# Query–key products in quarter tiles of the PE array, two steps per visit

## The chip, the cores and the metric

The kernel runs on one core of a Trainium2 chip. The metric is the device time of one launch in microseconds, as the median of three runs. Five engines work side by side, each through its own queue in order: PE (TensorE) multiplies matrices, with its weight loads shown apart as PEld; DVE (VectorE), ACT (ScalarE) and POOL (GpSimd) work on rows of numbers; SP (SyncE) issues the transfers. Matrix products land in PSUM, which has eight banks; everything else stands in SBUF.

## The reference

Four sequences of 576 positions go through windowed attention with eight heads of width 64 (a query sees the 128 latest keys, with a bias that falls with distance), then through a soft mixture of eight experts with four slots each, then through a dense layer with a squared ReLU. The change touches the attention alone.

```python
scores = scale * np.matmul(q, k.transpose(0, 1, 3, 2))
mask = (rel >= 0) & (rel < window)                  # rel = query position - key position
scores = np.where(mask, scores + bias[None], -1000000000.0)
scores = scores - np.max(scores, axis=-1, keepdims=True)
attn = np.exp(scores)
attn = attn / (np.sum(attn, axis=-1, keepdims=True) + 1e-09)
x = np.matmul(attn, v)
...
d = softmax of x @ phi over all 2304 tokens (per slot)
slot_out[e] = relu((d.T @ x)[e] @ w1[e]) @ w2[e]
x = softmax of x @ phi over the 32 slots (per token) @ slot_out
h = relu(x @ w_in); out = h * h @ w_out
```

## The kernel before

**Units, chunks, steps.** A unit `u` is one sequence and one pair of heads; there are 16. Its 576 queries are cut into nine chunks `c` of 64. The two heads of a pair lie on partitions 0 to 63 and 64 to 127. One chunk sees at most 192 keys (64 in the first chunk, 128 in the second). A step `t` handles two chunks, so there are 72 steps, 4.5 for each unit; `info[2 * t + i]` names the chunk `i` of step `t`.

**The stages of a step**, each in a function of its name:

- `emit_S(t)`, L157 to L163: one product for each chunk. The stationary operand is `zq`, 128 by 128: the queries of head 0 in the upper left quarter, those of head 1 in the lower right one, and zeros in the other two, so that one product gives both heads. The result stands in one PSUM bank for the step, chunk 0 in columns 0 to 191, chunk 1 from column 256 on. There are three such banks (tag `S`). Every fp32 product is shown as two PE instructions.
- `emit_max(t)`, L165: on DVE, one custom instruction for each chunk adds the bias table `tbl`, writes the scores into one of five buffers `pbuf[t % 5]` and takes the row minimum of the negated scores.
- `emit_exp(t)`, L176: on ACT, the exponential with its row sum.
- `emit_add(t)` and `emit_norm(t)`, L183 to L194: DVE adds 1e-9 to the two sums and takes their reciprocals; POOL multiplies the two chunks by them.
- `emit_T(t)`, L198: PE turns the step's probabilities, up to two 128 by 128 transposes into a bank `tp` and one or two into a bank `tq`. Both come from the tag `T`, which has three banks and also holds `xb`, `X`, `Y` and `R`.
- `emit_evac(t, 0)` copies `tp` into `ptb` on ACT, `emit_evac(t, 1)` copies `tq` on DVE, mostly in two pieces (L235, L237).
- `emit_PV(u)`, L239: when a unit's blocks are there, PE multiplies them with the values, in two halves of 64 array columns (`xa`, `xb`). `emit_xT` copies the result on ACT; `emit_xn` turns it again (five transposes into `X` and `Y`, L279 and L281), copied by DVE (L283) and ACT. After each fourth unit come the router's products `L` (32-column tiles, L267 and L272, a bank of their own with the tag `B`) and the sums of its softmax (`emit_d0` to `emit_d4`).

**The order** is written out by hand in the loop over `t` (L394 to L426): in step `t` PE does `emit_S(t + 1)`, then `emit_T(t - LT)` with `LT = 3`, then a due `emit_PV`. DVE does `emit_max(t)`, `emit_add(t - 1)` with the reciprocal, then `emit_evac(t - 3, 1)`; ACT does `emit_evac(t - 3, 0)` and then `emit_exp(t)`. A tile is reused only when all its readers are through, so an engine that runs ahead waits there.

**Transfers.** All loads are issued on SP. When `emit_S` has passed a unit's last chunk, the queries and keys of unit `u + 2` are loaded into the buffers of unit `u` (two loads for the queries, one for each half, in pieces of 64 numbers, since `zq` has zeros in between; one for the keys), and then one expert weight of 1 MB into a ring of 19 (two weights at `u` 2 and 6). For unit 0 the host has laid out the zeros itself (`z0`).

After the attention come the expert products (L567, L659), which run on weights from that ring, and the dense layer (L692, L735).

## Time and profile before

| what | value |
|---|---|
| median of three runs | 422.15 us (421.33 to 423.01) |
| the profiled execution, own time | 423.25 us |
| its span in the trace | 421.5 us |
| attention loop, first `emit_PV` to last | 16.28 us to 137.74 us |
| expert products | 148.2 us to 178.7 us |
| granted TensorE clock over the span | 0.994 |

The page shows, for each engine, how long it was busy; a busy PE includes the pipeline's overlap, so how densely it works is read from the distance between the starts of its rows. The profiled execution took 1.1 us more than the median, so what is said of the span's parts holds for the median within that.

### The profile page before, as it was taken

To read this page: it belongs to the slowest core of one execution; us is meant where nothing else is said; L and a number is where in the kernel's file an instruction comes from. 1 tells how busy PE (TensorE), PEld (TensorE's weight loads), DVE (VectorE), ACT (ScalarE), POOL (GpSimd) and SP (SyncE) were. 2 spreads that over 40 slices of the span, in tenths; PEclk is the share of its full clock that TensorE was granted. 3 is DMA by queue.
4 is the path that set the end of the run, shared out by engine and by line. 5 is a ranking of instruction groups with operands and counts; after the bars stand their busy time and mean duration, and the time that the engine had idled before them with its cause. 6 is when DMAs were issued, how large, how long until landed. Compare 5 with 4: busy or idle time off the path is not lost.

```text
span 421.5 us, 7942 instructions
## 1 busy us (share of the span) xinstructions
PE 400.4 (95%) x2623; PEld 306.7 (73%) x2623; DVE 293.4 (70%) x966; ACT 249.7 (59%) x761; POOL 94.6 (22%) x193
## 2 busy tenths in 40 slices
PE   5999997999999999978999999999999999999996
PEld 4878866878867633356778788787878888888885
DVE  6887777778788426587868768677676676548445
ACT  3888876778777402057766766666666645435341
POOL 4445334244334010146112210111100000000000
PEclk9999999999999999999999999999999999999999
DMA  7979769869686799999602202000000012004004
GB/s 215 307 276 305 261 218 323 218 194 313 223 287 233 264 425 423 412 409 408 255 0 101 100 2 100 2 0 0 2 1 2 1 64 87 0 2 150 0 2 150
DMA packets 35514, 70.95 MB, mean 168 GB/s; under 512 B 19856, under 2 KB 21008, under 8 KB 31376
## 3 DMA queue, kind: packets, MB, share of 16 engines
q1 hardware_dynamic: 35328, 70.30, 47.7%
q8 instruction: 21, 0.34, 0.4%
q14 instruction: 21, 0.17, 0.1%
q10 hardware_dynamic: 144, 0.13, 0.1%
HBM read 65.70 MB, written 4.72 MB: 167 GB/s over the span
## 4 chain that ended last, share of the span: by engine, by line
PE 51%; DVE 2%; issue 1%; POOL 1%; ACT 1%; DVEq 0%; POOLq 0%
PE acc L735 45%; PE h L692 4%; PE MX L644 1%; DVE psum L753 1%; PE MY L650 1%; POOL arena_y L605 1%; DVE arena_y L621 1%; DVE arena_y L619 0%; ACT whl L637 0%; DVE Mst L653 0%; DVE arena_co L623 0%; ACT psum L745 0%; ACT siT L745 0%; DVE arena_gh L721 0%; DVEq L896 0%
## 5 line engine op out<-in xcount | busy, mean ns | idle before, releaser
L735 PE MATMUL acc<-whl,arena_gh 128*128 128x512 f32 x864 | 214.4, 396 | 2.3 <-DVE arena_gh L721 1.8
L735 PEld LDWEIGHTS acc<-whl,arena_gh 128*128 128x128 f32 x864 | 159.9, 189 | 34.8 <-issue 2.8
L721 DVE TENSOR_TENSOR arena_gh<-hT,arena_gh 128x384 fp32r<-128x384 f32 (+1 forms) x95 | 52.7, 555 | 38.5 <-ACT arena_gh L717 34.1
L194 POOL TENSOR_SCALAR p<-p,st 128x192 f32<-128x192 f32 (+1 forms) x142 | 56.1, 408 | 77.0 <-PE s L162 20.2
L704 ACT ACTIVATE acc<-h 128x384 f32<-128x384 f32 (+2 forms) x49 | 23.8, 485 | 75.0 <-PE h L692 75.0
L181 ACT ACTIVATE p<-p,st 128x192 f32<-128x192 f32 (+1 forms) x144 | 61.3, 428 | 8.0 <-DVE st L170 7.3
L162 PE MATMUL s<-kt,zq 128*128 128x192 f32 (+2 forms) x288 | 58.8, 328 | 7.4 <-DMA kt<-in_k_dram 7.0
L605 POOL TENSOR_SCALAR arena_y<-f 128x512 f32<-128x512 f32 x32 | 27.9, 875 | 120.7 <-DVE arena_cin L623 59.0
L162 PEld LDWEIGHTS s<-kt,zq 128*128 128x128 f32 x288 | 44.8, 195 | 10.1 <-DMA zq<-in_z_dram 4.6
L237 DVE COPY ptb<-tq 64x128 f32<-64x128 f32 x128 | 35.4, 281 | 22.1 <-PE tq L215 18.9
L170 DVE CUSTOM_DVE_ANT_0 p<-s,tbl 128x192 f32<-128x192 f32 (+1 forms) x144 | 41.6, 324 | 2.3 <-PE s L162 1.8
L235 ACT ACTIVATE ptb<-tp 128x256 f32<-128x256 f32 (+1 forms) x72 | 25.3, 351 | 19.4 <-PE tp L213 18.1
L247 PE MATMUL xa<-ptb,vt 128*64 128x256 f32 (+1 forms) x256 | 27.8, 359 | 0.0
L213 PE MATMUL tp<-cs,p 128*128 128x128 f32 x128 | 26.4, 277 | 1.3 <-DVE ptb L237 0.7
L181 ACT ACTIVATION_READ_ACCUMULATOR p<-p,st 128x1 f32 x144 | 27.2, 189 | 0.0
L692 PE MATMUL h<-cst_sb,Mst 128*128 128x384 f32 x96 | 25.2, 341 | 1.9 <-DVE Mst L653 1.8
L713 DVE TENSOR_TENSOR hT<-acc 128x384 f32<-128x384 f32 (+1 forms) x18 | 10.2, 566 | 23.4 <-ACT acc L704 23.4
L717 ACT ACTIVATE arena_gh<-acc 128x384 fp32r<-128x384 f32 (+2 forms) x49 | 24.9, 508 | 0.6
L717 ACT ACTIVATE arena_gh<-hT 128x384 fp32r<-128x384 f32 x48 | 24.9, 518 | 0.6
L621 DVE SCALAR_TENSOR_TENSOR arena_y<-f,arena_y 128x512 int32<-128x512 int32 x32 | 24.1, 753 | 1.1
L247 PEld LDWEIGHTS xa<-ptb,vt 128*64 128x64 f32 x256 | 17.0, 136 | 9.6 <-issue 2.4
L692 PEld LDWEIGHTS h<-cst_sb,Mst 128*128 128x128 f32 x96 | 18.1, 190 | 7.1 <-DVE Mst L653 3.3
(171 smaller groups left out, 475.3 us busy)
## 6 DMA issues: line engine op xcount, KB each, us to landing
w_w<-in_w_dram SPq DMA_DIRECT2D x32, 1024.0 KB, 8.1
f<-in_w_in_dram SPq DMA_DIRECT2D x16, 512.0 KB, 10.2
f<-in_w_out_dram SPq DMA_DIRECT2D x16, 512.0 KB, 10.2
vt<-in_v_dram SPq DMA_DIRECT2D x16, 320.0 KB, 6.2
zq<-in_q_dram SPq DMA_DIRECT2D x30, 144.0 KB, 4.3
kt<-in_k_dram SPq DMA_DIRECT2D x15, 288.0 KB, 4.4
out_dram<-psum SPq DMA_DIRECT2D x11, 256.0 KB, 2.1
out_dram<-xn_all SPq DMA_DIRECT2D x4, 256.0 KB, 2.1
```

The costliest lines, as they stand in the source:

```text
L162: pe.matmul(out=sb_t[t][:, 256 * i:256 * i + n], lhsT=zq[u % NQ][:, c].rearrange("p a b -> p (a b)"), rhs=kt_t[u][:, 64 * c + 64 - n:64 * ...
L170: dve.tensor_tensor_reduce(out=p, in0=sb_t[t][:, 256 * i:256 * i + n], in1=tbl[:, 192 * pr + 192 - n:192 * pr + 192], scale=-0.125, scalar ...
L181: act.activation(out=p, in_=p, func=AF.Exp, bias=st[:, i:i + 1], scale=-1.0, accum_out=st[:, 2 + i:3 + i])
L194: eng.tensor_scalar(out=p, in0=p, scalar1=st[:, 4 + i:5 + i], scalar2=0.0, op0=ALU.mult, op1=ALU.add)
L237: dve.tensor_copy(out=dst, in_=src)
L247: pe.matmul(out=out, lhsT=v_t[u][:, j, po:po + 64], rhs=pt[:, a:b, po:po + 64], start=(j == 0 or (j == 3 and a == 2)), stop=(j == 4 or (j ...
L605: pool.tensor_scalar(out=y[:, a].bitcast(F32), in0=t[:, a, :, 1].bitcast(F32), scalar1=2.0 ** -112, scalar2=0.0, op0=ALU.mult, op1=ALU.add)
L621: dve.scalar_tensor_tensor(out=y[:, h], in0=t[:, h, :, 1], scalar=-0x80000000, in1=y[:, h], op0=ALU.bitwise_and, op1=ALU.bitwise_or)
L692: pe.matmul(out=hb[hf][:, 0:HB], lhsT=Mst[:, 128 * f:128 * f + 128], rhs=cst_sb[:, c0:c0 + HB], start=True, stop=True)
L717: act.activation(out=lo_t[i][1][hf][:, 0, cl], in_=rbuf[hf][:, cl], func=AF.Square)
L721: eng.tensor_tensor(out=gh[hf][:, 1, cl], in0=g[hf][:, cl], in1=gh[hf][:, 0, cl].bitcast(F32), op=ALU.subtract)
L735: pe.matmul(out=acc_t[s], lhsT=gh[:, x, c0:c0 + 128], rhs=w[:, f % 2, y, :], start=(f in firsts and a == 0), stop=(f in lasts and a == 2))
```

## The change

`emit_S` is called in even steps alone, for two steps at once (four chunks), two steps ahead. The queries are loaded as they are (`qt`, 128 by 576), without zeros. Each chunk takes two products, one for each head, with a stationary operand of 64 by 64 in one quarter of the array: the rows of head `h`, and the columns `64 * (h ^ w)`. `w` is 0 or 1 by the chunk's place in `pbuf`; with `w = 1` the two heads come out swapped, and the result stands in the second bank of a pair. There are two pairs of banks instead of three single banks. The bias table gets a second, swapped copy, and `emit_PV` finds its columns through a new function `cols`.

The sums of two steps are added to and inverted in one DVE instruction each, over four columns, in even steps; POOL normalizes four chunks after that. `LT` becomes 4. The router's `L` takes its bank from the tag `T`, whose number stays three. The double weight loads move from `u` 2 and 6 to 7, 11 and 13, and one of the extra loads at the end of the attention comes two steps sooner.

```diff
-LT = 3
+LT = 4
...
-    NBUF = {"S": 3, "T": 3, "xa": 1, "B": 1}
+    NBUF = {"S": 1, "T": 3, "xa": 1}
...
+    def pair(name):
+        return psum[0].tile([128, 2, 512], F32, tag="S", name=name, bufs=2)
...
     def emit_S(t):
-        sb_t[t] = bank("S", "s")
-        st_t[t] = apool.tile([128, 6], F32, tag="st", name="st", bufs=4)
-        for i in range(2):
-            u, c, n, e = info[2 * t + i]
-            pe.matmul(out=sb_t[t][:, 256 * i:256 * i + n], lhsT=zq[u % NQ][:, c].rearrange("p a b -> p (a b)"),
-                      rhs=kt_t[u][:, 64 * c + 64 - n:64 * c + 64], start=True, stop=True)
+        sb_t[t] = sb_t[t + 1] = pair("s")
+        st_t[t] = st_t[t + 1] = apool.tile([128, 12], F32, tag="st", name="st", bufs=3)
+        for x in range(2):
+            for i in range(2):
+                u, c, n, e = info[2 * t + 2 * x + i]
+                w = e // 192
+                for h in range(2):
+                    r, o = 64 * h, 64 * (h ^ w)
+                    pe.matmul(out=sb_t[t][o:o + 64, w, 256 * x:256 * x + n], lhsT=qt_t[u][r:r + 64, 64 * c:64 * c + 64],
+                              rhs=kt_t[u][r:r + 64, 64 * c + 64 - n:64 * c + 64], start=True, stop=True,
+                              tile_position=(r, o), skip_group_check=True)
...
     def emit_add(t):
         st = st_t[t]
-        dve.tensor_scalar(out=st[:, 2:4], in0=st[:, 2:4], scalar1=1e-9, scalar2=None, op0=ALU.add)
+        dve.tensor_scalar(out=st[:, 4:8], in0=st[:, 4:8], scalar1=1e-9, scalar2=None, op0=ALU.add)
+        dve.reciprocal(out=st[:, 8:12], in_=st[:, 4:8])
...
+    def cols(u, j, h, a, b):
+        ap = ptb[:, jblk(u, j) + a:jblk(u, j) + b, 0:64]
+        same = u % 2 == 1 and j == 0 and a == 0
+        first = 64 * (1 - h) if same else 64 * h
+        step = 128 if same else 128 + 64 * (1 - 2 * h)
...
-            for a, b in ((0, 4),) if j < 3 else ((0, 2), (2, 3)) if j == 3 else ((0, 1),):
+            for a, b in ((0, 2), (2, 4)) if u % 2 and j == 0 else ((0, 4),) if j < 3 else ((0, 2), (2, 3)) if j == 3 else ((0, 1),):
...
-            L_t[b] = bank("B", "L")
+            L_t[b] = bank("T", "L")
...
-        if t + 1 < NS:
-            emit_S(t + 1)
-            for u, c, n, e in info[2 * t + 2:2 * t + 4]:
+        if t % 2 == 0 and t + 2 < NS:
+            emit_S(t + 2)
+            for u, c, n, e in info[2 * t + 4:2 * t + 8]:
                 if c == NCH - 1:
                     if u + NQ < NU:
                         load_q(u + NQ)
-                    for _ in range(2 if u in (2, 6) else 1):
+                        load_k(u + NQ)
+                    for _ in range(2 if u in (7, 11, 13) else 1):
                         load_next_w()
...
-        if 0 <= t - 1 < NS:
-            emit_add(t - 1)
+        if t % 2 == 0 and 0 < t <= NS:
+            emit_add(t - 2)
         if t < NS:
             emit_exp(t)
-        if 0 <= t - 1 < NS:
+        if t % 2 == 0 and 0 < t <= NS:
+            emit_norm(t - 2)
             emit_norm(t - 1)
...
-        if t == NS - 2:
+        if t == NS - 4:
             zt.close()
             load_extra(1)
```

How the order of PE changes is seen at the same place in the program, the second unit: first the kernel before. `s` is the product of queries and keys, `tp` and `tq` are the two banks of a step's transposes.

```order
L162 MATMUL s_564<-kt_394,zq0_90 128x192 x2
L213 MATMUL tp_568<-cs_66,p0_93 128x128 x2
L215 MATMUL tq_569<-cs_66,p0_93 128x128
L162 MATMUL s_584<-kt_394,zq0_90 128x192 x2
L213 MATMUL tp_588<-cs_66,p1_94 128x128 x2
L215 MATMUL tq_589<-cs_66,p1_94 128x128
L162 MATMUL s_604<-kt_394,zq0_90 128x192 x2
L213 MATMUL tp_608<-cs_66,p2_95 128x128 x2
L215 MATMUL tq_609<-cs_66,p2_95 128x128
```

And the changed kernel on PE, two steps with their visit and the next visit (`X` and `Y` are the transposes of a finished unit):

```order
L167 MATMUL s_596<-kt_456,qt_454 64x192 x2
L221 MATMUL tp_612<-cs_66,p1_92 128x128 x2
L223 MATMUL tq_613<-cs_66,p1_92 128x128
L221 MATMUL tp_630<-cs_66,p2_93 128x128 x2
L223 MATMUL tq_631<-cs_66,p2_93 128x128
L297 MATMUL X_642<-cs_66,xT2_99 128x128 x4
L299 MATMUL Y_647<-cs_66,xT2_99 128x128
L167 MATMUL s_651<-kt_456,qt_454 64x192 x8
```

Products and transposes alternated step by step; now eight products stand together, and the transposes of two steps follow one another with no product between them.

On DVE, before, the last chunk of the second unit and the first chunk of the third: one step (the ISA rows of 64 to 192 columns are the row minima, the narrow ones read their result out):

```order
L170 ISA p3_96,st_389<-s_388,tbl_92 128x192
L170 ISA st_389 128x1
L170 ISA p3_96,st_389<-s_388,tbl_92 128x64
L170 ISA st_389 128x1
L185 TENSOR_SCALAR st_360<-st_360 128x2
L189 RECIPROCAL st_360<-st_360 128x2
L237 COPY ptb_98<-tq_437 64x128 x2
```

And on DVE after the change, two steps, the same chunks and the two that follow:

```order
L176 ISA p3_94,st_332<-s_331,tbl_90 128x192
L176 ISA st_332 128x1
L176 ISA p3_94,st_332<-s_331,tbl_90 128x64
L176 ISA st_332 128x1
L245 COPY ptb_96<-tq_415 64x128
L176 ISA p4_95,st_378<-s_377,tbl_90 128x128
L176 ISA st_378 128x1
L176 ISA p4_95,st_378<-s_377,tbl_90 128x192
L176 ISA st_378 128x1
L192 TENSOR_SCALAR st_332<-st_332 128x4
L193 RECIPROCAL st_332<-st_332 128x4
L245 COPY ptb_96<-tq_461 64x128 x2
```

The pair of small instructions on the sums stands in every second step, and works on four columns; the copies of `tq` keep their place behind each step's minima.

## Rows read from the trace of the kernel before

**Rows 1.** The page, part 1: engine, busy us, share of the span, instructions.

```profile
PE 400.4 (95%) x2623; PEld 306.7 (73%) x2623; DVE 293.4 (70%) x966; ACT 249.7 (59%) x761; POOL 94.6 (22%) x193
```

**Rows 2.** Stretches: length, then each engine's busy us, clock, DMA share, GB/s.

```profile
16.28:31.35 15.07, 14.33 (x121) 12.09 (x121) 12.23 (x73) 12.33 (x52) 7.12 (x18) 1.00 0.88 283
64.53:73.61 9.08, 6.71 (x57) 5.51 (x56) 6.90 (x41) 6.10 (x27) 4.77 (x12) 1.00 1.07 322
16.28:137.74 121.46, 115.71 (x1055) 93.08 (x1054) 95.14 (x541) 92.64 (x386) 51.50 (x130) 1.00 0.81 259
148.20:180.00 31.80, 31.77 (x283) 11.03 (x283) 14.58 (x46) 4.81 (x12) 4.58 (x5) 1.00 1.01 419
200.00:422.00 222.00, 216.41 (x1052) 175.31 (x1050) 150.87 (x274) 126.45 (x285) 19.77 (x22) 1.00 0.13 49
```

**Rows 3.** Timeline of PE: start us, us until the last end, line, tiles, count.

```profile
102.46 0.38 PE L213 MATMUL tp<-cs,p 128*128 128x128 f32 x2
102.68 0.27 PE L215 MATMUL tq<-cs,p 128*128 128x128 f32 x1
102.79 0.82 PE L162 MATMUL s<-kt,zq 128*128 128x192 f32 x4
103.44 0.38 PE L213 MATMUL tp<-cs,p 128*128 128x128 f32 x2
103.66 0.27 PE L215 MATMUL tq<-cs,p 128*128 128x128 f32 x1
```

**Rows 4.** Timeline of DVE over the same steps (brackets: idle before, releaser).

```profile
102.99 0.59 DVE L237 COPY ptb<-tq 64x128 f32<-64x128 f32 x2 [0.94 <-PE tq L215]
103.50 0.34 DVE L170 CUSTOM_DVE_ANT_0 p<-s,tbl 128x192 f32<-128x192 f32 x1
...
103.78 0.34 DVE L170 CUSTOM_DVE_ANT_0 p<-s,tbl 128x192 f32<-128x192 f32 x1
...
104.06 0.16 DVE L185 TENSOR_SCALAR st<-st 128x2 f32<-128x2 f32 x1
...
104.44 0.59 DVE L237 COPY ptb<-tq 64x128 f32<-64x128 f32 x2
104.96 0.34 DVE L170 CUSTOM_DVE_ANT_0 p<-s,tbl 128x192 f32<-128x192 f32 x1
```

**Rows 5.** Timeline of ACT over the same steps: copy, then the second exponential.

```profile
102.88 0.38 ACT L235 ACTIVATE ptb<-tp 128x256 f32<-128x256 f32 x1 [0.58 <-PE tp L213]
...
103.88 0.37 ACT L235 ACTIVATE ptb<-tp 128x256 f32<-128x256 f32 x1
```

**Rows 6.** Timeline of PE around one product with the values.

```profile
64.32 0.27 PE L221 MATMUL tq<-cs,p 128*128 128x128 f32 x1
64.53 1.73 PE L247 MATMUL xa<-ptb,vt 128*64 128x256 f32 x16
66.09 0.40 PE L247 MATMUL xb<-ptb,vt 128*64 128x64 f32 x8
66.42 0.92 PE L162 MATMUL s<-kt,zq 128*128 128x192 f32 x4
67.17 0.38 PE L213 MATMUL tp<-cs,p 128*128 128x128 f32 x2
```

**Rows 7.** Timeline of PE around the router's products, four tiles of 32 columns.

```profile
42.46 1.08 PE L267 MATMUL L<-xT,phi_sb 128*32 128x128 f32 x32
43.36 0.61 PE L272 MATMUL L<-xT,phi_sb 128*32 128x64 f32 x8
```

**Rows 8.** Timeline of DVE: copy of a unit's transposes, and the next step.

```profile
98.45 0.69 DVE L283 COPY xn_all<-X 128x512 f32<-128x512 f32 x1
99.06 0.35 DVE L170 CUSTOM_DVE_ANT_0 p<-s,tbl 128x192 f32<-128x192 f32 x1
```

**Rows 9.** Timeline of PE: the long wait in the stretch 64.53 to 73.61.

```profile
73.05 0.41 PE L162 MATMUL s<-kt,zq 128*128 128x64 f32 x2 [2.10 <-DMA kt<-in_k_dram]
```

**Rows 10.** The page, part 3: packets of the whole span.

```profile
DMA packets 35514, 70.95 MB, mean 168 GB/s; under 512 B 19856, under 2 KB 21008, under 8 KB 31376
```

More of the change, by code (lines that the diff above doesn't have):

```diff
@@ L24, with attn_moe_relu2_kernel @@
 RING = 19
[L25 removed]
+LT = 4
 @with_exitstack
[L29 removed]
+def attn_moe_relu2_kernel(ctx: ExitStack, tc: tile.TileContext, q, k, v, phi, w1, w2, w_in, w_out, bias, cst, out):
     nc = tc.nc
@@ L94, in keep_warm @@
     def keep_warm(tag, n):
-        b = bank(tag, "warm")
+        b = bank(tag, "warm") if tag in NBUF else Sbank[1]
         for _ in range(n):
@@ L114, in attn_moe_relu2_kernel @@
     NQ = 2
-    zq = [zpool.tile([128, NCH, 2, 64], F32, name=f"zq{i}") for i in range(NQ)]
-    tbl = ppool.tile([128, 768], BF16, name="tbl")
+    tbl = ppool.tile([128, NPAIR, 2, 192], BF16, name="tbl")
     NP = 5
@@ L237, in emit_evac @@
                 dve.tensor_copy(out=dst, in_=src)
+    def cols(u, j, h, a, b):
[3 more added lines that the diff above has]
+        step = 128 if same else 128 + 64 * (1 - 2 * h)
+        dims = [[256, (b - a) // 2], [step, 2], [1, 64]] if b - a > 1 else [[1, 64]]
+        assert not same or b - a == 2
+        return bass.AP(tensor=ap.tensor, offset=ap.offset + first, ap=[list(ap.ap[0])] + dims)
     def emit_PV(u):
@@ L461, in attn_moe_relu2_kernel @@
     pool.memset(siT, 0.0)
-    W = bank("B", "W")
+    Sp = pair("sp")
+    Sbank = [Sp[:, 0], Sp[:, 1]]
+    W = pair("W")[:, 0]
     for bb in range(4):
         pe.transpose(W[:, 128 * bb:128 * bb + 128], lgT[:, bb, 0:128], ident)
-    G = bank("S", "G")
+    G = Sbank[0]
     pe.matmul(out=G[:, 0:4], lhsT=rep, rhs=bm, start=True, stop=True)
@@ L877, in _layout @@
     for pr in range(NPAIR):
-        slope = 2.0 ** -(2.0 * pr + p // 64 + 1.0)
-        bias[:, 192 * pr:192 * pr + 192] = np.where(ok, -8.0 * slope[:, None] * rel, -8.0e9)
+        for w in range(2):
+            slope = 2.0 ** -(2.0 * pr + (p // 64 ^ w) + 1.0)
+            bias[:, pr, w] = np.where(ok, -8.0 * slope[:, None] * rel, -8.0e9)
     cst[:, 0:128] = np.eye(128, dtype=np.float32)
```

67 lines of the change are left out of this document (28 added, 39 removed).

## The prediction

> **What bounds the kernel now.** I read the page's busy shares first, then the stretches, then the timeline of each engine inside the stretch that the change touches. PE is busy for 95% of the span [rows 1], but the span has three parts with different limits. In the expert products PE is full (31.77 of 31.80 us) while the transfers run at a share of 1.01, and in the dense part PE has 216.41 of 222 us [rows 2]; both begin when the attention ends, and no instruction of theirs changes. So the change is decided in the attention loop, 121.46 us from the first product with the values to the last, which is 67 steps [rows 2].
>
> There the row to look at is the stretch 16.28 to 31.35: nine steps, two units, without the router's work, in 15.07 us, or 1.67 us a step [rows 2]. What does an engine need for nine steps? On PE, from start to start, a step's products take 0.65 us (102.79 to 103.44), its two tp transposes 0.22 and tq 0.11 [rows 3]: 0.98 us. A unit's product with the values takes 1.89 us (64.53 to 66.42) and 0.10 us more before it, since 0.21 lies between tq and xa where 0.11 lies between tq and s [rows 3, 6]. Its five transposes X and Y take 5 x 0.11 = 0.55. Nine steps hold two of each: 9 x 0.98 + 2 x 1.99 + 2 x 0.55 = 13.9 us. On DVE a step is 1.46 us (103.50 to 104.96) [rows 4], and a unit's copy of X 0.61 (98.45 to 99.06) [rows 8]: 9 x 1.46 + 2 x 0.61 = 14.4 us, some 0.4 less for the short first chunks. So **two engines are nearly full at once**, PE with 13.9 and DVE with 14.0 of 15.07 us. ACT is busy for 12.33 us, POOL for 7.12 [rows 2]. A cut on PE alone would change little; this change cuts both.
>
> **Products in quarters.** Two steps' products cost 2 x 0.65 = 1.30 us of PE. Four products of 64 by 64 at a time would need four passes of a quarter of that 0.65, 0.65 us a visit. That tiles work at the same time is seen for columns: 32 instructions of the router, four tiles of 32 columns, start within 0.90 us (42.46 to 43.36), four of them per 0.11 us, the time of one transpose of the same width [rows 3, 7]; and the two halves of xa run as pairs [rows 6]. No row of before shows tiles that split the array's rows. I take full overlap, 0.65, with 1.30 as the other end. What is new is two changes of tile shape for each visit: the 0.10 us before xa, and 0.10 more on the first group of s after xb (0.75 us from 66.42 to 67.17, against 0.65) [rows 3, 6]. That makes 0.20 to 0.40 us a visit; I take 0.30. A visit then costs 0.95 us, 0.35 less, and nine steps (4.5 visits) 1.6 us less of PE. Where a product with the values stands next to a visit, one change of shape was there already; the odd units' extra pair of short products leaves the columns as they are.
>
> **Sums of two steps.** One TENSOR_SCALAR and RECIPROCAL in two steps fall away, 0.38 us (104.06 to 104.44) [rows 4]: 1.7 us of DVE in nine steps. Wider by two columns costs nothing that a row shows. POOL gets its four multiplications in one go; it has half its time free, and the lag of four steps leaves two steps between the sums and the transposes, as before.
>
> If all else flowed as before, both full engines would lose 1.6 to 1.7 of 15.07 us: 67 / 9 x 1.65 = **12 us** at most.
>
> **The new closed loop.** The visit of step t needs a free pair of banks, so the minima of step t - 1 must be through. On DVE these stand behind the copies of the tq that PE made right after the visit before. PE waits at the visit, with the transposes of two steps and a due product with the values queued behind it; ACT waits for their tp, DVE for their tq. The loop, from the first product of a visit: transposes at 0.65 + 0.20 = 0.85; tq 0.22 later, 1.07; its copy begins 0.31 after tq (102.68 to 102.99), 1.38; the two copies take 0.51, 1.89; the two minima end 0.62 after the first starts (103.50 to 103.78 + 0.34), 2.51 [rows 3, 4]; about 0.1 to wake PE: 2.6 us. Against 2 x 1.46 on DVE that is a gain, but the rest adds to it. With a product with the values in the two steps PE needs 0.85 + 0.33 + 1.99 + 0.33 + 0.10 = 3.6 us, and 3.8 when it comes after the second step: there the transposes of two steps stand together, and the second tq takes the bank of the first tp, which ACT gives back 0.31 + 0.38 us after that [rows 5], some 0.3 late. With X and Y the copy of X (0.61) comes into the loop, or Y waits for a bank that ACT copies behind its exponentials (a copy and two short exponentials take 1.00 us, 102.88 to 103.88) [rows 5, 8]: 3.2 to 3.4. Nine steps are two of the first kind, two of the second and half a plain one: 2 x 3.7 + 2 x 3.3 + 0.5 x 2.6 = 15.3, less 0.3 for the short chunks: 15.0 us. **By this sum nothing is gained.**
>
> How far may such a sum be trusted? Made the same way for before (two steps with the values 2.97, two with X 2.07, five plain ones 1.46, less 0.3) it gives 17.1, and 15.07 were measured: engines work ahead into each other's steps and take back 12%. After the change less of that is possible, since the loop closes every two steps. I take a third of it, 4%, off: 14.35 us, 0.7 less than before, times 67 / 9: **-5.3 us**. The ends are -12 (above) and -0.5 (nothing taken back).
>
> **The rest.** The router's L now holds one of the three T banks, so X and Y of that step wait; on the other side L lies in the loop's shadow. A batch's softmax puts DVE work as long as X's copy (0.69) into the loop. Three batches, taken together **+0.8 us**, from -2 to +3. In the stretch 64.53 to 73.61 PE waited 2.10 us for keys while the transfers had a share of 1.07 [rows 2, 9], behind two weights that SP had issued one after the other. The double loads move, and the queries, until now in 256-byte pieces (19856 of 35514 packets are under 512 bytes [rows 10]), come in whole rows. I take **-1.9 us**, from 0 to -2.1; at u 7 the keys of unit 10 are still queued behind two weights. One step more of lag at the start against fewer bytes before the second visit, and a bank less at the end: **+0.7 us**, from -1 to +2. A nineteenth weight in the ring hides behind a full PE. PE's longer waits should not cost clock: it stayed at 1.00 in the stretch with the 2.10 us [rows 2].
>
> The sum: -5.3 + 0.8 - 1.9 + 0.7 = -5.7 us. The profiled execution would go from 423.25 to 417.6, the median from 422.15 to **416.4 us**.
>
> **The rivals.** *Quarters take turns* (the change does not do what it says). A visit would take 1.30 + 0.30, 0.65 more, straight into the loop: 36 x 0.65 = 23 us, some 435 to 440 us. For it: no row shows row tiles, and the quarters of one chunk write the same bank. The Trainium skill, "TensorEngine Tiling (Array Packing)", section "Restrictions and Gotchas", says that different row tiles cannot access the same PSUM bank simultaneously; by that rule the time is the one just given. No run here shows it; the skill's page "TensorE: Matmul & The Clock Gate", Part 3, on the other hand reports 10.6 times the speed for 16 tiles in rows and columns. Against it: column tiles that share a bank overlap fully [rows 7].
>
> *The loop is longer than its rows* (slower). Place: PE at the visit, waiting for DVE's minima, and at the second tq, waiting for ACT. If nothing is taken back, the changes of shape cost their dear 0.40 (0.45 in nine steps) and the bank's 0.3 us is lost in each plain or X pair too, nine steps take 15.9, and the end is 422.15 + 6.2 - 0.4 = 428 us. It decides from 15.13 us for nine steps on (with 0.4 gained elsewhere). *Nothing is taken back, but nothing more is lost:* 15.0 us, 421 us. *The engines' sums hold:* -12 - 0.4, 410 us.
>
> **How the numbers follow.** The forecast, 412 to 420 us: 0.48. Engines' sums, under 412: 0.12. About no change, 420 to 424: 0.18. Loop longer, 424 to 430: 0.14. Quarters in turn: 0.08. A measurement of this kernel can tell about 0.5%, 2.1 us, from no change: faster 0.60, same 0.18, slower 0.22. The range, 408 to 429, leaves out the quarters in turn and the outer ends of the two cases beside it.
>
> **What would show it.** Right: sixteen instructions of s within about 0.75 us on PE, waits of PE on DVE's minima that did not exist before, nine steps near 14.4 us, the stretch from the first to the last product with the values near 116 us, no wait of 2 us for keys, and expert and dense parts as long as before. Wrong: s spread over 1.3 us a visit; PE as full as before, which would mean that the loop has slack; or PE idle for over 1 us in plain pairs, which would mean that ACT's banks and not DVE set the loop.

## The result and the profile after

| | median, us | runs, us |
|---|---|---|
| the kernel before, same chip | 422.31 | 421.04 to 424.96 |
| the changed kernel | 426.09 | 423.52 to 430.48 |
| ratio | 1.0097 | 95% interval 1.007 to 1.0123 |

The change makes the kernel 0.97% slower. The forecast was 416.4 us, faster by 1.4%: the sign was wrong, though the time lies within the range 408 to 429. The profiled execution of the changed kernel took 425.98 us with a span of 424.2; that of the kernel before had 423.25 and 421.5. So the two traces differ by 2.7 us, and the medians by 3.8.

The page of the changed kernel, parts 1 and 2, answers to [rows 1, 10]:

```profile
PE 395.6 (93%) x2943; PEld 285.5 (67%) x2943; DVE 286.9 (68%) x894; ACT 249.2 (59%) x761; POOL 93.5 (22%) x191
...
DMA packets 19771, 70.87 MB, mean 167 GB/s; under 512 B 2192, under 2 KB 3344, under 8 KB 15632
```

PE has 4.8 us less to do, DVE 6.5 us less, and of 19856 packets under 512 bytes 2192 are left. The work became less, as forecast; the time did not. **Where it went** is read from one event that both kernels have, the first instruction of each product with the values (`xa`), and from the stages behind:

| event | before | after | later by |
|---|---|---|---|
| first `xa` | 16.28 | 19.29 | 3.01 |
| third | 31.35 | 36.34 | 4.99 |
| seventh | 64.53 | 69.54 | 5.01 |
| eleventh | 99.81 | 102.75 | 2.94 |
| fifteenth | 133.16 | 134.72 | 1.56 |
| sixteenth | 137.74 | 139.43 | 1.69 |
| first expert product | 148.22 | 150.45 | 2.23 |
| first product of the dense layer | 183.37 | 185.59 | 2.22 |
| end of the span | 421.5 | 424.2 | 2.7 |

The table says three things. All of the loss is there by the third unit, 5 us. From the third to the seventh, four units or 18 steps in the steady state, the two kernels take the same time. Later 2.1 us come back between the seventh and the eleventh, where the kernel before waits for keys [rows 9], and 1.4 us in the last units: the way from the fourteenth to the fifteenth takes 7.87 us, where the same place four units before takes 9.12. There the last visit, at 128.75, is already behind, and PE has only transposes and values left. The way from the last `xa` to the first expert product is 0.5 us longer, the dense layer 0.5.

**The steady state.** Stretches from the third to the seventh `xa`: first the kernel before, then the changed one (columns as in [rows 2]).

```profile
31.35:64.53 33.18, 32.24 (x294) 26.06 (x293) 26.07 (x150) 25.48 (x109) 14.21 (x36) 1.00 0.83 265
```

```profile
36.34:69.54 33.20, 30.50 (x373) 20.17 (x372) 24.31 (x131) 25.42 (x107) 14.08 (x36) 1.00 0.72 237
```

PE and DVE each lost 1.7 us of work in 33, and the stretch is as long as before. Idle time took the place of work. The changed kernel's PE behind a product with the values shows both what was gained and what it cost:

```profile
62.31 0.88 PE L167 MATMUL s<-kt,qt 64*64 64x192 f32 x16
63.12 0.44 PE L221 MATMUL tp<-cs,p 128*128 128x128 f32 x2
63.40 0.27 PE L223 MATMUL tq<-cs,p 128*128 128x128 f32 x1
63.51 0.38 PE L221 MATMUL tp<-cs,p 128*128 128x128 f32 x2
64.09 0.33 PE L223 MATMUL tq<-cs,p 128*128 128x128 f32 x1 [0.21 <-ACT ptb L243]
65.03 0.78 PE L167 MATMUL s<-kt,qt 64*64 64x64 f32 x16 [0.60 <-DVE st L176]
65.73 0.44 PE L221 MATMUL tp<-cs,p 128*128 128x128 f32 x2
```

Two steps' products, 16 instructions, take 0.81 us to the start of the next transposes, where two steps took 1.30 [rows 3] (each product is two instructions). The second `tq` of a pair waits for the bank that ACT gives back, and the next visit waits for DVE's minima: the waits that the prediction's closed loop named.

The prediction counted in nine steps without the router. Such a stretch of the changed kernel, and the nine steps with the router behind it, with what works on `s` alone (length, then busy us and instructions of PE, PEld and DVE, clock, DMA share, GB/s):

```profile
27.21:43.06 15.85, 4.29 (x80) 2.46 (x80) 5.17 (x19) 1.00 0.68 223
43.06:60.41 17.35, 3.39 (x64) 2.07 (x64) 4.95 (x18) 1.00 0.81 275
```

The two stretches hold five visits and four (80 and 64 instructions), since a visit comes in every second step. Moved by half a visit (0.5 us) they are about 15.4 and 17.8 us, an estimate, against 15.07 and 18.13 before. So nine plain steps became longer, and the stretch with the router shorter; only the 18 steps together, with nine visits, can be compared as they stand.

**The start.** PE of the changed kernel from 10 to 20 us:

```profile
10.21 0.38 PE L221 MATMUL tp<-cs,p 128*128 128x128 f32 x2
10.63 0.33 PE L223 MATMUL tq<-cs,p 128*128 128x128 f32 x1
11.23 0.56 PE L167 MATMUL s<-kt,qt 64*64 64x192 f32 x8 [0.27 <-DVE st L176]
13.44 0.70 PE L167 MATMUL s<-kt,qt 64*64 64x64 f32 x8 [1.64 <-DMA kt<-in_k_dram]
14.07 0.69 PE L221 MATMUL tp<-cs,p 128*128 128x128 f32 x2
14.55 0.42 PE L223 MATMUL tq<-cs,p 128*128 128x128 f32 x1
14.76 0.63 PE L221 MATMUL tp<-cs,p 128*128 128x128 f32 x2
15.23 0.47 PE L223 MATMUL tq<-cs,p 128*128 128x128 f32 x1
16.33 1.56 PE L167 MATMUL s<-kt,qt 64*64 64x192 f32 x16 [0.62 <-DVE st L176]
17.82 0.47 PE L221 MATMUL tp<-cs,p 128*128 128x128 f32 x1
```

And the two stretches, with the granted clock in the third column from the end:

```profile
10.00:15.00 5.00, 3.04 (x27) 1.96 (x26) 2.26 (x13) 2.33 (x11) 3.11 (x8) 0.83 1.00 376
15.00:20.00 5.00, 4.38 (x29) 2.64 (x29) 3.86 (x24) 3.87 (x19) 1.64 (x4) 0.50 0.66 261
```

The visit reaches the first chunks of unit 2 two steps ahead of its place in the kernel before and finds no keys: 1.64 us of waiting, with the transposes of two steps queued behind it, while the transfers run full (share 1.00). Behind the wait PE works at half rate: the granted clock is 0.50, the lower of its two levels (1.2 GHz), the visit at 16.33 takes 1.49 us to the next transposes instead of 0.81. In the kernel before the same stretch reads 1.00 and the same wait is 0.52 us.

### The profile page after: what moved, and what is told of

Same layout as the page of the kernel before. It is cut to its first block, busy times and chain, and to the rows that moved or that the text cites. A ratio compares the mean times of both kernels' runs of the same rounds, so it can differ in the third digit from the quotient of the medians.

```text
span 424.2 us, 8517 instructions
## 1 busy us (share of the span) xinstructions
PE 395.6 (93%) x2943; PEld 285.5 (67%) x2943; DVE 286.9 (68%) x894; ACT 249.2 (59%) x761; POOL 93.5 (22%) x191
## 2 busy tenths in 40 slices
DMA packets 19771, 70.87 MB, mean 167 GB/s; under 512 B 2192, under 2 KB 3344, under 8 KB 15632
## 3 DMA queue, kind: packets, MB, share of 16 engines
HBM read 65.60 MB, written 4.72 MB: 166 GB/s over the span
## 4 chain that ended last, share of the span: by engine, by line
PE 51%; DVE 2%; ACT 1%; issue 1%; DVEq 0%
PE acc L754 45%; PE h L711 4%; PE MX L663 1%; DVE psum L772 1%; PE MY L669 1%; DVE arena_y L640 0%; ACT whl L656 0%; DVE arena_gh L740 0%; DVE Mst L672 0%; DVE arena_y L638 0%; DVE arena_co L642 0%; ACT siT L764 0%; ACT psum L764 0%; DVEq L912 0%; ACT Mst L671 0%
## 5 line engine op out<-in xcount | busy, mean ns | idle before, releaser
L167 PE MATMUL s<-kt,qt 64*64 64x192 f32 (+2 forms) x576 | 34.2, 345 | 9.5 <-DMA kt<-in_k_dram 5.9
L167 PEld LDWEIGHTS s<-kt,qt 64*64 64x64 f32 x576 | 20.2, 144 | 16.9 <-DVE st L176 6.2
L221 PE MATMUL tp<-cs,p 128*128 128x128 f32 x128 | 28.9, 303 | 1.4 <-DVE stat L348 0.5
L265 PEld LDWEIGHTS xa<-ptb,vt 128*64 128x64 f32 x288 | 18.3, 138 | 8.5 <-issue 1.7
L221 PEld LDWEIGHTS tp<-cs,p 128*128 128x128 f32 x128 | 14.7, 144 | 13.7 <-issue 9.2
```

What stands on the lines that cost most here:

```text
L167: pe.matmul(out=sb_t[t][o:o + 64, w, 256 * x:256 * x + n], lhsT=qt_t[u][r:r + 64, 64 * c:64 * c + 64], rhs=kt_t[u][r:r + 64, 64 * c + 64 - ...
L221: pe.transpose(A[:, i, :], P[:, e:e + 128], ident)
L265: pe.matmul(out=out, lhsT=v_t[u][:, j, po:po + 64], rhs=cols(u, j, h, a, b), start=((j == 0 and a == 0) or (j == 3 and a == 2)), stop=(j = ...
```

## Experiments

The kernel before was run beside each set; its medians were 422.18 us (e1 to e4), 422.62 (e5 to e8), 422.78 (e9 to e11) and 422.85 (e12 to e14).

**The start or the loop.** Two theories stood: the start (late keys, then half rate), and the closed loop of visit, transposes, copy and minima in the steady state.

e1: the loads of the start in another order.

```diff
-    sp.dma_start(out=tbl[:, 1:]..., in_=bias[:, 384:])
+    sp.dma_start(out=tbl[:, 1]..., in_=bias[:, 384:768])
...
-    sp.dma_start(out=phi_sb, in_=phi)
-    load_v(1)
...
                         load_k(u + NQ)
+                    if u == 0:
+                        sp.dma_start(out=tbl[:, 2:]..., in_=bias[:, 768:])
+                        load_v(1)
+                        sp.dma_start(out=phi_sb, in_=phi)
```

> Only the order of loads at the start changes: the bias tables of pairs 2 and 3 (192 KB), the values of unit 1 (320 KB) and phi (64 KB) are issued after the queries and keys of unit 2 instead of ahead of them. Theory 'start': the loss of the change sits before the first product with the values (19.29 us after, 16.28 us before), in the 1.64 us wait for the keys of unit 2 and in the granted clock of 0.83 and 0.50 that followed. 576 KB less ahead at about 360 GB/s bring these keys 1.6 us sooner; if the clock then stays at 1.00 from 10 to 20 us, the first product with the values starts at 16.8 to 17.5 and the time falls from 426.1 to 423.5 to 424.5, with a smaller spread of runs. Middle case: the wait goes but PE still waits for the minima and the clock falls all the same: 18.3, about 425. Rival 'loop': the loss sits in the steady loop, the start is hidden by it: 426 +- 0.7.

423.48 us (422.65 to 425.95), ratio to before 1.0038 (1.002 to 1.0057), against 1.0097 for the change as it was: 2.6 us of the 3.8 are gone, in the range of the start theory. The wait of 1.64 us for the keys is gone from the trace. The profiled execution, though, was the slowest of the ten (425.95). It fits the middle case of the expectation: its third `xa` stands at 36.12, only 0.2 us sooner than in the changed kernel, and it shows the rate apart from the wait:

```profile
11.04 0.63 PE L221 MATMUL tp<-cs,p 128*128 128x128 f32 x2
11.46 0.42 PE L223 MATMUL tq<-cs,p 128*128 128x128 f32 x1
12.10 1.33 PE L167 MATMUL s<-kt,qt 64*64 64x192 f32 x16 [0.22 <-DVE st L176]
```

Two transposes take 0.42 us to the next, as at half rate, with its first `xa` at 18.58. So the low rate can come without that wait. How the faster executions gained their 2.6 us no trace shows; that the low rate comes in some executions and not in others would fit their spread.

e2: the transposes of even steps ahead of the visit.

```diff
+        if 0 <= t - LT < NS:
+            emit_T(t - LT)
         if t % 2 == 0 and t + 2 < NS:
             emit_S(t + 2)
...
-        if 0 <= t - LT < NS:
-            emit_T(t - LT)
         for a in side0.get(t, ()):
```

> Only the place of one call changes: in even steps PE makes the transposes of step t - 4 ahead of the products of steps t + 2 and t + 3, no longer behind them. Theory 'closed loop': the visit waits for the minima of step t - 1, these stand on DVE behind copies of a tq that PE made only after the visit before; with the transposes ahead of the visit the copy no longer hangs on it, and the nine-step stretches without router (15.85 us from 27.21 to 43.06, two units) fall to 14.3 to 14.8; first to last product with the values from 120.14 to 115 to 117, the time from 426.1 to 421 to 423. Rival 'PE and the banks': the time is set by PE's own work and by the three T banks that ACT gives back; the order within two steps does not matter: 120 +- 0.7, 425.5 to 426.7. Rival 'worse': the products come 0.33 us later behind the transposes and the minima starve: first to last 123, 429.

422.43 us, ratio 1.0004 (0.998 to 1.0027). The time is the one that the loop theory gave, but the trace contradicts the theory. Waits of PE for something over 18 steps, first in the changed kernel (from 36.34 to 69.54 us; engine, line, waited for, total, times, longest; `issue` is time for which the profile shows no releaser):

```profile
PE s L167 <- DVE st L176: 0.6, 1, 0.6
...
PEld tp L221 <- issue: 2.2, 8, 0.4
PEld s L167 <- DVE st L176: 1.4, 3, 0.8
PEld tq L223 <- ACT ptb L243: 1.3, 3, 0.4
...
PEld tp L221 <- POOL p L202: 0.7, 3, 0.3
```

then in e2 (32.34 to 65.60):

```profile
PE tp L221 <- ACT xnr L302: 0.5, 1, 0.5
PE tp L221 <- DVE ptb L245: 0.4, 1, 0.4
...
PEld tp L221 <- issue: 2.9, 7, 0.7
PEld tp L221 <- POOL p L202: 1.5, 4, 0.6
```

The visit no longer waits for the minima; the transposes wait instead, for POOL's normalization and for banks. And the stretch is no shorter:

```profile
32.34:65.60 33.26, 30.42 (x376) 20.17 (x372) 24.32 (x132) 25.33 (x108) 13.98 (x36) 1.00 0.72 247
```

33.26 us against 33.20. The gain is at the start, where the third `xa` stands at 32.34 instead of 36.34: the transposes are no longer queued behind the visit that waits for keys. The half rate is not gone: here PE shows it from 10.25 to about 14 us. The closed loop exists, and opening it moved the wait, not the time.

e3: both edits.

> The edits of the two runs before together. If the start and the loop are separate losses, the gains add: start theory 2 to 2.5 us and loop theory 3 to 5 us give 418.5 to 421, below the kernel before (422.3). If the loop theory is wrong: 423.5 to 425, as with the start alone. If both are wrong: 426.

421.55 us, ratio 0.9992 (0.9979 to 1.0006). Gains of 2.6 and 3.7 us did not add to 6.3 but to 4.5: both take back the same loss. The third `xa` is at 31.18, 0.2 us ahead of the kernel before, and the steady stretch is still 33.26 us. Without the start's loss the change is no slower than the kernel before, and no faster.

**What the quarters give, and what eats it.** The question is now why the steady state gains nothing. e4 to e7 take the change apart.

e4: the lag.

```diff
-LT = 4
+LT = 3
```

> The changed kernel with LT = 3 instead of 4, nothing else. Theory 'lag costs at the start': the first product with the values comes one step (1.5 to 1.7 us) sooner and the loop is unchanged: 424.5. Theory 'the lag of four is needed': with three the transposes of an odd step stand one step behind the joint normalization of four chunks on POOL (4 x 0.41 = 1.6 us after the sums), PE waits for POOL in every second step, 0.3 to 0.8 us each: first to last product with the values from 120.1 to 130 to 148 us, the time 435 to 452.

437.04 us, ratio 1.0353 (1.0332 to 1.0374): the lag of four is needed with joint sums. The four units take 35.93 us, and PE waits for POOL, ahead of its products 2.7 us, ahead of its weight loads 5.6 us:

```profile
PE tp L221 <- POOL p L202: 2.7, 4, 0.9
...
PEld tp L221 <- POOL p L202: 5.6, 10, 1.1
```

e5: the whole change without the quarters.

```diff
-                w = e // 192
-                for h in range(2):
-                    r, o = 64 * h, 64 * (h ^ w)
-                    pe.matmul(out=sb_t[t][o:o + 64, w, ...], lhsT=qt_t[u][r:r + 64, ...], rhs=kt_t[u][r:r + 64, ...], tile_position=(r, o))
+                pe.matmul(out=sb_t[t][:, e // 192, 256 * x:256 * x + n], lhsT=zq[u % NQ][:, c].rearrange("p a b -> p (a b)"),
+                          rhs=kt_t[u][:, 64 * c + 64 - n:64 * c + 64], start=True, stop=True)
```

> The kernel before with every part of the change but the quarters: two steps in one visit, pairs of banks, joint sums, lag of four, L in a T bank, the later double loads; the queries stay in the layout with zeros, and a visit is four products with a stationary operand of 128 by 128. A visit costs 1.30 us, against 0.65 + 0.27 for the quarters with their changes of shape as the trace of after shows them. Theory 'closed loop' (a visit, the transposes, the copy of tq and the minima follow one another): the 0.38 us go straight into each of 36 visits, 14 us, about 440. Rival 'PE's own time is not in the path': 425 to 428. Rival 'the quarters cost what they save' : 422 to 426.

439.33 us, ratio 1.0373 (1.0333 to 1.0413). Against the changed kernel the quarters are worth 13 us, and something else in the change costs as much. Not all of the 13 us is in the visits: the two traces are 14.4 us apart, and 5.5 of them are there by the third `xa` (41.84 against 36.34), where this version waits for keys too (1.11 us) and a granted clock of 0.66 is shown from 15 to 25 us. The steady stretch below is the cleaner measure.

e6: the lag alone, on the kernel before (`LT = 4`).

> The kernel before with LT = 4 instead of 3, nothing else. Theory 'one step more of lag costs a step at the start': 422.2 + 1.5 = 423.7. Rival 'more slack helps the loop': 419 to 421. Rival 'hidden': 422.2 +- 0.7.

426.32 us, ratio 1.008 (1.0051 to 1.011): one number changed in the kernel before costs about as much as the whole change. 1.4 us of it are at the first `xa` (17.64); the rest is in the loop (the four units from the third to the seventh take 0.97 us more), less what comes back because this trace has no wait of 2.1 us for keys.

e7: lag of four and joint sums, on the kernel before.

```diff
-        dve.tensor_scalar(out=st[:, 2:4], in0=st[:, 2:4], scalar1=1e-9, scalar2=None, op0=ALU.add)
+        dve.tensor_scalar(out=st[:, 4:8], in0=st[:, 4:8], scalar1=1e-9, scalar2=None, op0=ALU.add)
+        dve.reciprocal(out=st[:, 8:12], in_=st[:, 4:8])
...
-        if 0 <= t - 1 < NS:
-            emit_norm(t - 1)
+        if t % 2 == 0 and 0 < t <= NS:
+            emit_norm(t - 2)
+            emit_norm(t - 1)
```

> The kernel before with LT = 4 and the joint sums of two steps: one addition and one reciprocal on DVE fall away in two steps, 0.38 us, 0.19 us a step; products, visits and banks as before. Theory 'two full engines' (PE 13.9 and DVE 14.0 of 15.07 us in nine steps): a cut on DVE alone leaves PE, so against the lag of four alone it gives 0 to -3 us: 421 to 424. Rival 'DVE alone sets the loop': 67 x 0.19 = -12 us, 411. Rival 'POOL's four products in one go come too late for the transposes': slower than the lag of four alone, 425 or more.

425.57 us, ratio 1.0052 (1.0018 to 1.0086): 0.75 us less than the lag alone, which is inside the scatter of both.

Stretches of four units in e6, e7 and e5, in this order (of e7 from the seventh to the eleventh `xa`, since in its first four units PE waited once 1.7 us for keys):

```profile
33.18:67.33 34.15, 32.52 (x294) 26.05 (x293) 26.26 (x150) 25.53 (x108) 14.22 (x36) 1.00 0.84 267
```

```profile
68.36:102.07 33.71, 32.79 (x294) 26.14 (x293) 24.59 (x134) 25.61 (x110) 13.98 (x36) 1.00 0.74 237
```

```profile
41.84:78.45 36.61, 34.08 (x293) 26.30 (x292) 24.64 (x131) 25.35 (x107) 14.31 (x38) 1.00 0.72 221
```

With the two stretches shown above this gives the account of 18 steps in the steady state: 33.18 before; lag of four +0.97; joint sums -0.44; two-step visits with pairs of banks, `L` in a T bank and the later weights +2.90; quarters -3.41; 33.20 after. Each term is the difference of two traces along this one order of edits (e9 and e14 below show that the lag's price hangs on what else is there), and the -0.44 compares unlike stretches.

A visit was to get 1.30 - 0.92 = 0.38 us shorter by the quarters, and nine visits make 3.42. The 0.92 is a little low: a plain visit takes 0.96 us with its changes of tile shape (last section), 0.34 less than 1.30, and nine make 3.1. The 3.41 measured are all of that and a little more, so PE's time at the visit lies on the path in full. What the quarters need to pay off, two steps in one visit, costs nearly the same. The +2.90 is a bundle of four edits that was not taken apart. e5 has the two waits that the changed kernel has, ahead of weight loads 1.4 us for the minima and 1.3 us for the bank that ACT gives back, and e7 has neither; but e2 took the first of them away and gained nothing by it, so which part of the form costs the time is not shown.

**Why does the lag cost?** e10 moves the product with the values one step, with the lag of three, in the kernel before.

```diff
-        t0 = (NCH * u + 8) // 2 + LT
+        t0 = (NCH * u + 8) // 2 + LT + (u < NU - 1)
```

> The kernel before (LT = 3) with the product with the values and all that follows it one step later, for units 0 to 14; the lag of the transposes stays. Theory 'place against the short chunks': in the kernel before, PE does the short first chunks' products (0.44 us against 0.65) in the step just ahead of the product with the values; with a lag of four they come a step sooner, and this cost most of the 0.46 us in nine steps that the lag of four added to the kernel before. Here the product with the values moves in the same way, and the nine-step stretches without router go from 15.07 to 15.4 to 15.6, the time to 425 to 426. Rival 'the lag itself': the place does not matter, nine steps 15.07 +- 0.15, 422 to 423.5.

423.52 us, ratio 1.0014 (0.999 to 1.0038). Two units without router take 15.23 us (from 59.13 to 67.25 and 74.36), 0.2 more than before; the lag of four added 0.5 to such a stretch. So the place against the short chunks explains less than half of what the lag costs, and the time leans to the rival. The rest of the lag's price stays open.

**The keys.** e11: the kernel before with the double loads at other units.

```diff
-                    for _ in range(2 if u in (2, 6) else 1):
+                    for _ in range(2 if u in (7, 11, 13) else 1):
```

> The kernel before with the second weight loaded at units 7, 11 and 13 instead of 2 and 6, nothing else. Theory 'the wait for keys is on the path': the 2.10 us wait at 73.05 us goes, 420.2. Rival 'made up later, or another transfer is late in its place': 422.2 +- 0.7.

421.95 us, ratio 0.9963 (0.9937 to 0.9989). The wait of 2.10 us is gone, and the profiled span is 419.7 instead of 421.5. By the ratio it is 1.6 us, by the medians 0.8. The time alone lies in the range of the rival; the ratio's interval and the trace speak for the theory. So this term of the sum had its place right and its size roughly, and it is the one part of the change that is shown to pay by itself. The wait is not the same in all executions: e6, with the double loads in their old places, has none there.

**Is there a version that beats both?** e8: e3, with DVE's copy of `tq` behind the next step's minima.

```diff
+        if t < NS:
+            emit_max(t)
+        if 0 <= t - LT - 1 < NS:
+            emit_evac(t - LT - 1, 1)
         if 0 <= t - LT < NS:
             emit_T(t - LT)
...
-        if 0 <= t - LT < NS:
-            emit_evac(t - LT, 1)
```

> The version with both edits (transposes ahead of the visit, loads of the start in another order; 421.6 us), and on DVE the copy of a step's tq is put behind the minima of the next step. In that version DVE still waits 0.9 us at 59.23 us for a tq that PE makes behind a product with the values, while the scores for its next minima are ready. Theory 'DVE's place in the order': that wait goes, four units take 30.5 to 32 instead of 33.3 us, 410 to 417. Rival 'banks': a tq is held a step longer, the transposes of the next step but one wait for its bank, and PE loses what DVE gains: 421 to 424. Rival 'worse': the product with the values waits for the later copy, 0.6 us for each of 16: 430.

438.00 us, ratio 1.0338 (1.0294 to 1.0383). The wait of DVE did not go, it changed its line, from the copy (5.9 us in e3) to the minima, which now stand ahead of the copy; `X` comes late too:

```profile
DVE p L176 <- PE tq L223: 5.4, 3, 1.9
DVE xn_all L301 <- PE X L297: 2.2, 3, 1.4
```

The minima of a step write the buffer `pbuf` that the transposes of five steps before have to read, so they wait for the same transposes. What a sixth buffer would give was not run. A part of the loss is the clock: 0.96 was granted over this version's four units (32.46 to 70.58), and one `xa` in them took 2.41 us where 1.74 is usual.

e9: e3 with a lag of three and each step's own sums.

```diff
-LT = 4
+LT = 3
...
-        dve.tensor_scalar(out=st[:, 4:8], in0=st[:, 4:8], scalar1=1e-9, scalar2=None, op0=ALU.add)
-        dve.reciprocal(out=st[:, 8:12], in_=st[:, 4:8])
+        a = 4 + 2 * (t % 2)
+        dve.tensor_scalar(out=st[:, a:a + 2], in0=st[:, a:a + 2], scalar1=1e-9, scalar2=None, op0=ALU.add)
+        dve.reciprocal(out=st[:, a + 4:a + 6], in_=st[:, a:a + 2])
```

> The version with both edits (transposes ahead of the visit, start loads; 421.6 us), with LT = 3 and each step's own addition, reciprocal and normalization as in the kernel before; quarters, two-step visits and pairs stay. Theory 'the lag was the price': the fourth step of lag alone cost the kernel before 3.7 us and the joint sums gave back 0.75, so this version loses 3.0 us: 418.5 +- 1. Rival 'the visit two steps ahead needs the lag': PE, ahead by two steps, reaches the transposes of step t - 2 one visit (0.9 us) after the minima of step t - 1 are through, when POOL (0.4 us a chunk, after ACT and the sums) has just begun on that step; it waits 0.3 to 0.8 us in every second step and the loop gets 11 us or more longer: 432 or more.

421.01 us (420.34 to 421.85), ratio 0.9932 (0.9905 to 0.9959): faster than both kernels. Its steady stretch is clearly shorter than that of the others, though DVE has the work of the single sums back:

```profile
30.73:63.28 32.55, 30.12 (x374) 20.20 (x373) 26.12 (x150) 25.67 (x108) 14.23 (x37) 1.00 0.68 235
```

Its next four units take 33.07 us, so the gain is not steady. And a good part of its lead on the kernel before is the keys: e11, the kernel before with the later loads alone, ran beside it and took 421.95, so that the quarters with all that they need bring 0.9 us.

e14: the same exchange on the changed kernel, without the two edits.

> The changed kernel with LT = 3 and each step's own addition, reciprocal and normalization, as in the kernel before; the order (transposes behind the visit) and the loads of the start as in after. Theory 'the lag was the price': the same exchange was worth 0.5 us on the version with both edits (421.55 to 421.0) and should be worth up to 3.0 us here (the lag cost the kernel before 3.7, the joint sums gave back 0.75): 423 to 425.5. Rival 'the closed loop wants the lag': with the transposes behind the visit they reach POOL's output later, and PE does not wait for it: then 423 or less. Rival 'POOL late': the transposes of the odd step wait for POOL, 428 or more.

426.47 us, ratio 1.0086 (1.0058 to 1.0113), no different from the change, and between the ranges of the three theories. Its first `xa` is 2 us sooner (17.32), its steady stretch longer:

```profile
31.55:65.49 33.94, 30.87 (x373) 20.26 (x372) 26.41 (x150) 25.47 (x108) 14.23 (x36) 1.00 0.69 235
```

So the lag of three with single sums pays only where the transposes stand ahead of the visit.

**Dummies at the start.** e12: products on data that is there, in PE's waits of the changed kernel.

```diff
+    WARM = {3: 2, 5: 7, 7: 4}
...
+        if t in WARM:
+            for _ in range(WARM[t]):
+                pe.matmul(out=b[:, 0:128], lhsT=qt_t[w][:, 0:128], rhs=kt_t[w][:, 0:128], start=True, stop=True)
```

> The changed kernel with 13 added products of 128 by 128 whose result nobody reads, in PE's waits of the start: 2 before the visit of step 6, 7 before that of step 8 (where it waits for the keys of unit 2), 4 before that of step 10; loads and order as in after. Theory 'clock at the start': in after the transposes from 14.76 to 18.52 us start 0.21 us apart, those at 10.21 and from 25.37 on 0.11; PE had idled 1.64 us for the keys and 0.62 for the minima before. If the dummies keep the spacing at 0.11, the first product with the values comes at 17.3 to 17.8 instead of 19.29, the time falls by 1.5 to 2 us to 424.1 to 424.6, and the runs lie closer together (423.5 to 430.5 without). Rival 'the late keys alone': the spacing recovers but the chain waits for the keys and DVE all the same: 425.5 to 426.5. Rival 'the dummies are in the way': 427.

425.44 us, ratio 1.0057 (1.0029 to 1.0086), between the theories. The rate did recover:

```profile
12.90 1.76 PE L425 MATMUL warm<-kt,qt 128*128 128x128 f32 x14
14.59 0.76 PE L167 MATMUL s<-kt,qt 64*64 64x192 f32 x16
15.28 0.44 PE L221 MATMUL tp<-cs,p 128*128 128x128 f32 x2
15.56 0.27 PE L223 MATMUL tq<-cs,p 128*128 128x128 f32 x1
...
19.11 1.74 PE L265 MATMUL xa<-ptb,vt 128*64 128x256 f32 x16
```

The transposes at 15.28 are back at 0.28 for two. But the dummies stood in the way: the first four took 1.15 us at half rate (9.14 to 10.29) ahead of a visit that in the changed kernel had run without a wait, the 14 another 1.69. The first `xa` came only 0.18 us sooner. How the start's loss divides between the keys and the rate, this run doesn't tell.

e13: six dummies before the first visit of e9, on zeros.

> The fastest version (transposes ahead of the visit, start loads, LT = 3 with each step's own sums; 421.0 us) with six added products of 128 by 128 on buffers of zeros, whose result nobody reads, before the first visit, while PE waits for the first keys (3.58 us). Theory 'PE starts at the lower rate and rises with work': the first full visit, whose passes of 192 columns start 0.27 to 0.32 us apart until 8.7 us, runs at 0.16, the first product with the values comes 0.5 to 1 us sooner than 15.75: 420 to 420.5. Rival 'DVE and the loads set the start': 421.0 +- 0.5.

420.77 us, ratio 0.9942 (0.9919 to 0.9965), the same as e9. The dummies did not raise the rate: behind them two transposes still took 0.43 us at 9.58, where e9 without dummies had 0.41 at 9.13 and full rate soon after.

```profile
9.58 0.64 PE L222 MATMUL tp<-cs,p 128*128 128x128 f32 x2
10.01 0.42 PE L224 MATMUL tq<-cs,p 128*128 128x128 f32 x1
```

## Why the prediction was wrong

**Quarters: right.** Four products run at a time. A visit with its changes of shape was put at 0.95 us and takes 0.96: 0.81 to the next transposes, against 0.65 in pure passes, and the rest around it (below). The rival "quarters take turns" (1.60 us a visit) is out, and e5 shows the saving in the time, 3.41 us in four units for 3.1 to 3.4 worked out.

**Sums: nearly right in the rows, but DVE was not full.** Their rows in 18 steps fell from 6.0 to 3.1 us, 2.9 where the prediction had 3.4. In the time of those 18 steps the runs show 0.4 us of it (e6 to e7, from unlike stretches). The premise failed: the prediction multiplied one dense step of DVE and got 14.0 of 15.07 us. Over that very stretch, 16.28 to 31.35 of the kernel before, DVE waited 2.3 us for a `tq` (total, times, longest), which leaves it 12.8:

```profile
DVE ptb L237 <- PE tq L215: 2.3, 2, 1.3
```

So one engine was nearly full, PE, and a cut on DVE was worth little.

**Steady loop, -5.3 us: this is the step that failed.** By its sum of rows nothing was to be gained, and nothing was: 33.18 and 33.20 us in four units. The prediction then took 4% off, a third of what the same way of summing had overstated for the kernel before. No row bore out the third. That the sum came so near has luck in it: its 15.0 us were for nine steps without the router, which take about 15.4, and the stretch with the router made up for it. What the forecast had left out is the price of the form: +2.90 us in four units for two-step visits with pairs of banks, with the same instructions. That this is the lost freedom to work ahead fits, but was inferred; no run separates it.

**"The lag of four steps leaves two steps between the sums and the transposes, as before": a term put at nothing that costs.** In the kernel before, the lag alone costs 3.7 us (e6), 0.97 of it in four units. The prediction looked at what waits for the lag's data and allowed only for one step at the start. Why the loop gets longer with it stays open (e10).

**Router, +0.8: not there.** Two units with the router take about 17.8 us (17.35 with half a visit added) against 18.13 before, two without it about 15.4 against 15.07. The sum over a batch is zero, and neither row was forecast.

**Keys, -1.9: right in the trace.** 2.07 us less from the seventh to the eleventh `xa`; in the time e11 shows 0.8 to 1.6 us.

**Start and tail, +0.7, and a clock that stays at 1.00: mis-sized, and this gave the wrong sign.** It was 5.0 us by the third `xa`, and 0.5 each on the way to the expert products and in the dense layer: 6.0 where 0.7 was forecast. The loop with its router was to give back 4.5 us and gave 1.2, all of it in the last units. These two errors, 5.3 and 3.3, less 0.2 that the keys gave more than forecast, are the 8.4 us between the forecast difference of the traces (-5.7) and the measured one (+2.7). A visit that looks two steps ahead needs the keys of unit 2 two steps sooner, when the transfers were already full; fewer bytes in small packets were counted, the earlier need was not. e1 and e2 take most of it back in two ways, by 2.6 and 3.7 us; with both (e3) the time is that of the kernel before.

**The rivals.** "The loop is longer than its rows" forecast 428 us within 424 to 430, and 426.1 came. Its nine steps of 15.9 us seem to come too (15.85), but only because that stretch holds five visits. Its place was PE at the visit in the steady loop, and e2 shows that this wait is exchanged for others at no cost, while the loss was at the start: the right number by the wrong mechanism, so by luck. (Its parts as given, 0.45 and two and a half times 0.3 on 15.0, make 16.2 for nine steps and some 430 us, not 15.9 and 428.) "Nothing is taken back" describes four units of the steady state, though not the nine plain steps for which it was worked out.

**The signs named beforehand:** 16 instructions of `s` within 0.75 us: 0.81 with the exit. New waits for the minima: there. No wait of 2 us for keys: right in the loop, wrong at 13.44. Nine steps near 14.4 us: 15.85, about 15.4 with four and a half visits. First to last `xa` near 116 us: 120.14. Expert products as long as before: yes.

## What to carry to other kernels

Where two engines alternate in one order, count what a change does to the freedom to work ahead as well as what it removes: here 3.4 us of saved passes and 0.4 of saved sums in four units paid for 2.9 us of the two-step form and 1.0 of lag. Before an engine is called full, look for its waits over the same stretch. If a sum by hand says that nothing is gained, believe it until a row shows what takes time back. Compare stretches that hold the same number of visits. And whatever looks further ahead needs its first data sooner: check the start's transfers for it before the steady state.

## What the runs showed of the hardware

**Row tiles and one bank.** The four quarters split the array's rows and columns, and the two of one chunk lie on different rows and write the same PSUM bank, in different partitions. They ran four at a time: 16 instructions and the way out took 0.81 us. One after another, at the 0.16 us that each of the four full ones took before (0.65 in all [rows 3]), they would take 2.6 us. The Trainium skill, "TensorEngine Tiling (Array Packing)", "Restrictions and Gotchas", says that different row tiles cannot access the same bank simultaneously. Here they did, at full speed; for tiles that write different partitions the measurement decides against the rule.

**A change of tile shape costs on three sides.** Timeline of PE in e2:

```profile
59.80 0.27 PE L223 MATMUL tq<-cs,p 128*128 128x128 f32 x1
60.01 0.88 PE L167 MATMUL s<-kt,qt 64*64 64x192 f32 x16
60.82 0.44 PE L221 MATMUL tp<-cs,p 128*128 128x128 f32 x2
61.09 0.27 PE L223 MATMUL tq<-cs,p 128*128 128x128 f32 x1
```

0.21 us from `tq` to the visit where 0.11 is usual, 0.81 through the visit where four passes take 0.65, and 0.27 for the first two transposes where 0.22 is usual: about 0.3 us for each visit, 0.96 us in all.

**The rate at the start.** In e1 the stretch from 10 to 15 us shows a granted clock of 1.00, while two transposes took 0.42 us as in the changed kernel at 0.50. At the start of these traces the rate is better read from the distance of like instructions than from that column.

```profile
10.00:15.00 5.00, 4.78 (x35) 2.81 (x28) 3.08 (x17) 3.04 (x14) 2.85 (x8) 1.00 1.00 367
```
